# The last group's output-projection rows loaded as two tiles instead of one, in a decode attention block

## The chip, the cores and the metric

One core of a Trainium2 chip runs the whole kernel. The metric is the device time in microseconds (us) of one execution; medians of several runs are given. The profile is of one execution; its span is about 1.8 us shorter than the time, because it leaves out what lies around the first and the last instruction. In the views, PE is TensorE (matrix products), DVE is VectorE, ACT is ScalarE, and SP (SyncE) issues the loads.

Where times from different profiles are compared, they are counted from one event that all kernels share: the start of the last eight products with v ("from the last v" below). Such a figure is the difference of two times that are printed to 0.01 us, so it can be off by 0.01.

## The reference, cut to what matters

```python
h = _layernorm(x) * (1 + ca) + sa
x = x + ga * _A_ref(h, A_k_cache, A_v_cache, A_wq, A_wo)   # attention, 4 x 32 heads, 4096 keys of 128
h = _layernorm(x) * (1 + cb) + sb
x = x + gb * _B_ref(h, B_w_in, B_w_sp, B_b_sp, B_w_out)    # gated MLP
# in _A_ref:  o = softmax(q k^T) v ;  return o.reshape(B, 1, H * Dh) @ wo
# in _B_ref:  z = gelu(x @ w_in); z1 * (w_sp * layernorm(z2) + b_sp) @ w_out
```

The k and v caches are 134 MB each and every byte is used once. They are streamed in 32 steps: eight groups of four heads, times four batch rows. wo, w_in and w_out are small.

## The kernel before: the parts that matter

All large loads are issued on one queue (SP). At the last step the queue gets the last v tile in five parts (1/2, 1/4, 1/8, 1/16, 1/16), then the last group's rows of wo (512 KB), then w_in as two tiles (1344 and 448 KB) and w_out as two tiles (512 and 384 KB):

```python
st["v", i] = load_v(i)                                   # five parts when i is the last step
if i == NQ - 1:
    nc.sync.dma_start(out=st["wo", G - 1], in_=wo_v[G - 1])
    for a, (j0, j1) in enumerate(WJS):
        nc.sync.dma_start(out=win[a], in_=win_v[:, j0:j1, :])
    for a, (j0, j1) in enumerate(JFS):                   # JFS = [(0, 4), (4, 7)]
        nc.sync.dma_start(out=wout[a], in_=wout_v[a])
```

After the last products with v, the attention output oT of the last group meets wo in 16 small products (four heads by four column blocks):

```python
for hl in range(NH):
    for jo in range(J):
        nc.tensor.matmul(attn_ps[:, jo, :], lhsT=wo_g[:, hl, jo * P:(jo + 1) * P], rhs=oT[:, hl, :], ...)
```

What follows is one serial chain of small steps (cut): `x1b` (residual), the second layernorm, `h`; the products with w_in (`z_ps`); gelu, `u`; the third layernorm with an activation table load before its `rstd` (one over the standard deviation); the products with w_out (`y_ps`); `gwb` and `q`, and at the second step of `q` the two branches meet:

```python
for a, (j0, j1) in enumerate(JFS):                       # 28 products: 16 with wout[0], 12 with wout[1]
    ... nc.tensor.matmul(y_ps[:, jo], lhsT=wout[a][...], rhs=u[:, jf], ...)
nc.vector.tensor_tensor(out=gwb, in0=y_ps, in1=gwb, op=ALU.mult)
nc.vector.tensor_tensor(out=q, in0=gwb[:, :, 0], in1=gwb[:, :, 1], op=ALU.add)
nc.vector.tensor_tensor(out=q, in0=q, in1=bc(rstd, J), op=ALU.mult)      # y branch and rstd branch meet
... # add, transpose by one product, copy, and a DMA of the 4 KB output
```

## Time and profile before

| What | Value | Where it is read |
|---|---|---|
| time | 667.54 us, 3 runs (667.51 to 667.61) | the timed runs |
| bytes moved | 283 MB, 425 GB/s over the span | the page |
| last v products start | 653.43 us | timeline |
| products with wo | 654.74 to 655.33 us | timeline |
| last w_out tile lands | 661.26 us (issued 650.96, 10.3 us to landing) | groups by tile |
| last step of q starts | 662.39 us | timeline |
| output issued | 663.57 us | timeline |

The page of the kernel before. Its third part gives, for each DMA queue, packets, MB and share of the 16 DMA engines' time; its fourth the chain of work that ended last, by engine.

```profile
DMA packets 12733, 283.17 MB, mean 425 GB/s; under 512 B 1432, under 2 KB 1952, under 8 KB 4000
...
q1 hardware_dynamic: 12624, 282.73, 98.8%
...
DMA 62%; PE 24%; DVE 12%; ACT 1%; issue 0%; SPq 0%; DVEq 0%
```

The kernel is a stream from HBM. What this change can move lies after the stream's last v bytes. The timeline of that tail (start, duration, engine, line, operation, tiles, number; in brackets what the engine waited for):

```profile
653.43 0.38 PE L363 MATMUL zo_ps<-P_1_109,vt 128*128 128x4 bf16 x8 [0.24 <-DMA vt<-in_A_v_cache_dram]
...
654.74 0.59 PE L400 MATMUL attn_ps<-oT,wo_g 128*128 128x4 bf16 x16 [0.93 <-DMA wo_g<-in_A_wo_dram]
655.37 0.17 DVE L467 TENSOR_TENSOR x1b<-attn_ps,modT 128x16 f32<-128x16 f32 x1 [1.35 <-PE attn_ps L400]
...
658.08 0.17 DVE L479 TENSOR_TENSOR h<-xs,modT 128x16 bf16<-128x16 f32 x1
...
658.40 1.08 PE L492 MATMUL z_ps<-h,win_434 128*128 128x4 bf16 x30 [1.75 <-DVE h L479]
...
659.34 0.35 PE L492 MATMUL z_ps<-h,win_435 128*128 128x4 bf16 x7
...
661.30 0.49 PE L515 MATMUL y_ps<-u,wout_437 128*128 128x12 bf16 x12
...
661.83 0.21 DVE L524 TENSOR_TENSOR gwb<-y_ps,gwb 128x48 f32<-128x48 f32 x1 [0.21 <-PE y_ps L515]
662.07 0.17 DVE L528 TENSOR_TENSOR q<-gwb 128x16 f32<-128x16 f32 x1
662.15 0.20 ACT L171 ACTIVATE rstd_ln_4194<-rstd_ln_4194 128x4 f32<-128x4 f32 x1
...
662.39 0.18 DVE L529 TENSOR_TENSOR q<-q,rstd_ln_4194 128x16 f32<-128x16 f32 x1
```

All 16 products with wo wait for one landing. Near the end two branches run side by side: the y branch (w_out landing, 12 products, gwb, first q) is done at 662.24 and rstd at 662.35. The chain that ended last names the one that released the meeting point (start, duration, what):

```profile
631.94 22.76 DMA wo_g<-in_A_wo_dram
654.69 0.05 issue
654.74 0.60 PE attn_ps L400 x16
...
660.52 1.28 ACT L508
...
661.82 0.31 ACT rstd_ln_4194 L170
...
662.15 0.21 ACT rstd_ln_4194 L171
...
662.39 0.19 DVE q L529
```

Before the change the chain runs from wo through compute and the activation table load (L508) to rstd.

### The profile page before, as it was taken

The page shows a single profiled execution, that of the slowest core. Times are in us where ns is not written, and L with a number is a line of the kernel's source. Part 1 is how long each engine was busy: PE and PEld are TensorE (multiplying, and loading weights), DVE is VectorE, ACT ScalarE, POOL GpSimd, SP SyncE. Part 2 cuts the span into 40 slices and gives each one's busy share as a digit, 9 for nine tenths or more (in the row PEclk, how much of TensorE's full clock was granted, in tenths as well). Part 3 has the DMA queues.
Part 4 walks back from the last instruction along what each step waited for, and adds up shares of the span by engine and source line. Part 5 has one row for each costly group of instructions (what it writes and reads, how often), then busy time and mean ns, then how long its engine had stood idle before and what let it go on. Part 6 is the DMA issues. An engine that isn't in the chain of part 4 may idle for free.

```text
span 665.9 us, 6937 instructions
## 1 busy us (share of the span) xinstructions
PE 410.8 (62%) x3023; PEld 203.3 (31%) x3024; DVE 402.9 (60%) x475; ACT 41.3 (6%) x115; POOL 4.7 (1%) x21
## 2 busy tenths in 40 slices
PE   2557776645676555577665577655566655557774
PEld 2223332222333222233222333222233322223344
DVE  2177766665556665556576556767555757655762
ACT  1200000000000000000000000000000000000002
POOL 2000000000000000000000000000000000000000
PEclk9988876767888667887677887766788766788885
DMA  9999999999999999999999999999999999999995
GB/s 378 433 425 432 438 434 429 427 440 432 429 428 439 432 430 428 437 428 436 429 435 428 436 431 434 426 436 433 434 431 431 434 434 426 437 432 435 426 417 228
DMA packets 12733, 283.17 MB, mean 425 GB/s; under 512 B 1432, under 2 KB 1952, under 8 KB 4000
## 3 DMA queue, kind: packets, MB, share of 16 engines
q1 hardware_dynamic: 12624, 282.73, 98.8%
q8 instruction: 23, 0.38, 0.2%
q14 instruction: 6, 0.05, 0.0%
q0 software_dynamic: 64, 0.00, 0.0%
q10 hardware_dynamic: 16, 0.01, 0.0%
HBM read 282.73 MB, written 0.00 MB: 425 GB/s over the span
## 4 chain that ended last, share of the span: by engine, by line
DMA 62%; PE 24%; DVE 12%; ACT 1%; issue 0%; SPq 0%; DVEq 0%
DMA kt<-in_A_k_cache_dram 58%; PE s_ps L281 23%; DVE kt L276 11%; DMA wo_g<-in_A_wo_dram 3%; SPq L92 0%; PE big L341 0%; PE z_ps L492 0%; DVE S L290 0%; ACT L508 0%; ACT E L311 0%; DVE P_1_109 L314 0%; DVE P_0_105 L314 0%; PE small L155 0%; PE attn_ps L400 0%; DVE mT L300 0%
## 5 line engine op out<-in xcount | busy, mean ns | idle before, releaser
L281 PE MATMUL s_ps<-kt,ident 128*128 128x512 bf16 x1024 | 289.8, 454 | 190.0 <-DVE kt L276 190.0
L276 DVE TENSOR_TENSOR kt<-kt,qbc 128x8192 bf16<-128x8192 bf16 x64 | 282.7, 4420 | 87.3 <-DMA kt<-in_A_k_cache_dram 73.4
L281 PEld LDWEIGHTS <-ident 128*128 128x128 bf16 x1024 | 115.5, 113 | 352.8 <-issue 224.2
L290 DVE TENSOR_REDUCE S<-s_ps 128x64 f32<-128x512 f32 x64 | 44.3, 692 | 120.6 <-PE s_ps L281 120.6
L354 PE MATMUL zo_ps<-sel,osb 128*128 128x4 f32 x248 | 33.1, 257 | 26.6 <-ACT osb L347 26.6
L311 ACT ACTIVATE E<-S,nm 128x128 f32<-128x128 f32 x32 | 12.8, 401 | 564.2 <-DVE nm L308 564.2
L354 PEld LDWEIGHTS zo_ps<-sel,osb 128*128 128x128 f32 x248 | 30.5, 194 | 38.4 <-ACT osb L347 38.4
L341 PE MATMUL big<-vt,P_0_105 128*32 128x512 bf16 x352 | 21.0, 380 | 1.5 <-DMA vt<-in_A_v_cache_dram 1.5
L341 PE MATMUL big<-vt,P_1_109 128*32 128x512 bf16 x320 | 19.1, 381 | 0.0
L341 PE MATMUL big<-vt,P_2_113 128*32 128x512 bf16 x320 | 19.1, 380 | 0.0
L347 ACT COPY osb<-big 128x512 f32<-128x512 f32 x31 | 17.5, 566 | 20.0 <-PE big L341 20.0
L215 PE MATMUL big<-vt,hbc 128*32 128x512 bf16 x128 | 8.9, 445 | 4.9 <-DMA vt<-in_A_wq_dram 4.9
L314 DVE TENSOR_TENSOR P_1_109<-E,mask_99 128x512 bf16<-128x512 f32 x11 | 7.6, 693 | 6.8 <-ACT E L311 6.8
L314 DVE TENSOR_TENSOR P_0_105<-E,mask_99 128x512 bf16<-128x512 f32 x11 | 7.6, 693 | 6.7 <-ACT E L311 6.7
L341 PEld LDWEIGHTS <-P_0_105 128*32 128x32 bf16 x352 | 8.4, 96 | 8.9 <-DMA vt<-in_A_v_cache_dram 1.6
L314 DVE TENSOR_TENSOR P_2_113<-E,mask_99 128x512 bf16<-128x512 f32 x10 | 6.9, 693 | 6.2 <-ACT E L311 6.2
L400 PE MATMUL attn_ps<-oP,wo_g 128*128 128x4 bf16 x112 | 3.8, 165 | 10.5 <-DVE oP L397 10.5
L375 DVE TENSOR_TENSOR oT<-zo_ps,rz 128x4 bf16<-128x4 f32 x32 | 5.4, 168 | 7.4 <-PE zo_ps L363 6.3
L341 PEld LDWEIGHTS <-P_1_109 128*32 128x32 bf16 x320 | 7.6, 96 | 6.7
L341 PEld LDWEIGHTS <-P_2_113 128*32 128x32 bf16 x320 | 7.6, 96 | 6.7
L400 PEld LDWEIGHTS <-wo_g 128*128 128x128 bf16 x128 | 4.3, 97 | 11.5 <-issue 10.4
L308 DVE STREAM_TRANSPOSE nm<-hb 128x32 f32<-128x32 f32 x32 | 6.8, 211 | 1.1
(218 smaller groups left out, 130.7 us busy)
## 6 DMA issues: line engine op xcount, KB each, us to landing
kt<-in_A_k_cache_dram SPq DMA_DIRECT2D x31, 4096.0 KB, 26.0
vt<-in_A_v_cache_dram SPq DMA_DIRECT2D x31, 4096.0 KB, 33.8
vt<-in_A_wq_dram SPq DMA_DIRECT2D x1, 4096.0 KB, 20.4
wo_g<-in_A_wo_dram SPq DMA_DIRECT2D x8, 512.0 KB, 26.2
kt<-in_A_k_cache_dram SPq DMA_DIRECT2D x2, 2048.0 KB, 25.4
vt<-in_w_mod_dram SPq DMA_DIRECT2D x1, 3072.0 KB, 10.1
vt<-in_A_v_cache_dram SPq DMA_DIRECT2D x1, 2048.0 KB, 18.5
win_434<-in_B_w_in_dram SPq DMA_DIRECT2D x1, 1344.0 KB, 24.4
```

Of the source, the lines that this page charges most:

```text
L215: nc.tensor.matmul(qp[hl * R:(hl + 1) * R, 0:n], lhsT=hbc[:, j, b, :], rhs=wv[:, g0:g0 + n, hl, :], start=(j == 0), stop=(j == J - 1), til ...
L276: nc.vector.tensor_tensor(out=kt, in0=kt, in1=q[:, None, :].to_broadcast([P, HT, DH]), op=ALU.mult,)
L281: nc.tensor.matmul(ps, lhsT=ident, rhs=kt[:, :, cc * DC:(cc + 1) * DC], start=(cc == 0), stop=(cc == DH // DC - 1),)
L290: nc.vector.tensor_reduce(out=st["S", i][:, half * HT:(half + 1) * HT], in_=st.pop(("s", i, half)), axis=AX.X, op=ALU.add,)
L308: nc.vector.transpose(out=nm, in_=hb)
L311: nc.scalar.activation(out=E, in_=S, func=AF.Exp, bias=nm[:, 0:1], scale=att_scale, accum_out=rs,)
L314: nc.vector.tensor_tensor(out=P4[:, 0:NT, :], in0=E[:, :, None].to_broadcast([P, NT, NH]), in1=mask4[:, None, :].to_broadcast([P, NT, NH]) ...
L341: nc.tensor.matmul(po[32 * t:32 * t + 32], lhsT=P4[:, n0:n0 + 8, :], rhs=st["v", i][:, n0:n0 + 4, :], start=(u == 0), stop=(u == NU - 1), ...
L347: nc.scalar.copy(out=osb, in_=po)
L354: nc.tensor.matmul(st["o", i], lhsT=osb[:, n, :], rhs=sel[:, NH * n:NH * n + NH], start=(n == 0), stop=(n == 3),)
L375: nc.vector.tensor_tensor(out=oT[:, :, b], in0=st.pop(("o", i)), in1=rz, op=ALU.mult,)
L400: nc.tensor.matmul(attn_ps[:, jo, :], lhsT=wo_g[:, hl, jo * P:(jo + 1) * P], rhs=oT[:, hl, :], start=(g == 0 and hl == 0 and jo == 0), sto ...
```

## The change

The intent: with wo in two tiles of two heads each, the first eight products can run while the second tile is still under way.

```diff
-                            attn_ps[:, jo, :], lhsT=wo_g[:, hl, jo * P:(jo + 1) * P], rhs=oT[:, hl, :],
+                            attn_ps[:, jo, :],
+                            lhsT=(wo_g[:, hl] if g < G - 1 else wo_l[hl // 2][:, hl % 2])[
+                                :, jo * P:(jo + 1) * P],
+                            rhs=oT[:, hl, :],
 ...
+        wo_l = [wk.tile([P, NH // 2, D], BF16, name=f"wo_l{a}", bufs=1) for a in range(2)]
 ...
             if i == NQ - 1:
-                nc.sync.dma_start(out=st["wo", G - 1], in_=wo_v[G - 1])
+                for a in range(2):
+                    nc.sync.dma_start(
+                        out=wo_l[a], in_=wo_v[G - 1, :, a * NH // 2:(a + 1) * NH // 2],
+                    )
```

(The rest of the diff only keeps the old tile for the other seven groups.) The same bytes and the same products; one queue entry more.

More of the change, by code (lines that the diff above doesn't have):

```diff
@@ L384, in apply @@
                 oT = st.pop(("oT", g))
-                wo_g = st.pop(("wo", g))
                 if g < G - 1:
+                    wo_g = st.pop(("wo", g))
                     pp = psum_s.tile([P, NH, B], F32, name="small", bufs=1)
@@ L429 @@
                 g = quads[i][0]
-                st["wo", g] = wk.tile([P, NH, D], BF16, name="wo_g", bufs=2)
                 if g < G - 1:
+                    st["wo", g] = wk.tile([P, NH, D], BF16, name="wo_g", bufs=2)
                     nc.sync.dma_start(out=st["wo", g], in_=wo_w[g])
```

## The prediction

> **What bounds the kernel.** The page's queue part gives the SP queue 98.8% of the DMA time and 425 GB/s over the 665.9 us span: the kernel streams 283 MB, and DMA is 62% of the chain of waits. The instruction orders of both kernels differ only in the last queue entries and in the tile that the last 16 wo products read, so only the last 12 us (654 to 665.9) can move.
>
> **The tail before (timeline).** The last v part lands at about 653.4; oT is ready at 654.02 (653.85 + 0.17). wo_g lands at 654.70 (chain of waits). The 16 products run 654.74 to 655.33 (0.59 us). Then the second layernorm runs serially to h at 658.25, and the win products start at 658.37. Their first weight load waits for h and for the first win tile, which landed at 657.97 (633.57 + 24.4): h released it.
>
> **What the change does.** Same bytes, packets and products; one more DMA. wo took 1.31 us after the last v part, so the first half should land at about 654.05, just as oT is ready. Eight products (about 0.3 us) then run in the wait, and the other eight start at 654.74. attn_ps finishes at about 655.04: 0.29 us saved at the layernorm's start, and h at about 657.97.
>
> **How much survives.** Less, because the transfers behind wo come no earlier:
> - win, first tile, 657.97: h now meets it; products start near 658.08 (-0.29).
> - win, second tile: by bytes between its neighbours' landings about 659.04 (estimate); needed at 659.31 before, 659.02 now: even, 0 to 0.1 us lost.
> - wout, second tile: lands at 661.26 (650.96 + 10.3) and its weight load already started at 661.30, so this end is DMA-bound. y products end 661.79, gwb at 661.83, q at 662.07 to 662.24. The other input, rstd, came at 662.35. An earlier rstd gains only until 662.24: about 0.13 us.
>
> So I expect about 0.1 us: 0.29 us saved, the rest given back in waiting for wout.
>
> **Side effects.** Each queue entry waits for the landing eight entries earlier (instruction order). Now the first win tile waits for the v tile before the last (landed about 643.3) instead of the last k half (633.5). Its issue lasted until 644.02 anyway (10.45 us). The second win tile is issued at about 648.2 instead of 644.07, the wouts at 651 and 652.3 instead of 648.16 and 650.96. Their data flow 6 us later, so the queue should not run dry. The Trainium skill (DMA: Bandwidth & Descriptors, "Anatomy of one DMA") gives a fixed cost of about 2 us per DMA, mostly completion latency. Here it is hidden: the v parts of 512 and of twice 256 KB each filled about 1.23 us per 512 KB, no dearer when split; an extra DMA should cost under 0.05 us.
>
> **Prediction.** 667.4 us (before 667.54), range 666.7 to 668.1. Chances: faster by over 2% 0.005, within 0.99, slower 0.005.
>
> **What would show each step.** Right: two groups of eight wo products, the first starting near 654.1, ahead of the second landing; first x1b product at about 655.07 instead of 655.37; the last y products waiting for wout's second tile; span shorter by 0.05 to 0.2 us. Wrong: the first half landing with the second; win's landing releasing its products over 0.1 us late; wout landing later than 661.3.
>
> **What would make it wrong.** The later issues letting some DMA engines run dry (the windows show DMA share falling to 0.57 from 656 on, so the engines are uneven), delaying win or wout by up to 1 us; or a drift of 0.1% in the whole run's DMA rate, larger than the effect.

## The result, and the profile after

The changed kernel took 667.39 us (667.18 to 667.48, 6 runs), the kernel before beside it 667.51 us (667.38 to 667.61, 6 runs). The ratio is 0.9998 with a 95% interval of 0.9985 to 1.0011: the same.

The timeline of the changed kernel, the lines that answer to those of before:

```profile
653.03 0.37 PE L363 MATMUL zo_ps<-P_1_109,vt 128*128 128x4 bf16 x8 [0.26 <-DMA vt<-in_A_v_cache_dram]
...
653.69 0.37 PE L400 MATMUL attn_ps<-oT,wo_l_438 128*128 128x4 bf16 x8 [0.29 <-DMA wo_l_438<-in_A_wo_dram]
...
654.36 0.38 PE L400 MATMUL attn_ps<-oT,wo_l_439 128*128 128x4 bf16 x8 [0.30 <-DMA wo_l_439<-in_A_wo_dram]
654.78 0.17 DVE L474 TENSOR_TENSOR x1b<-attn_ps,modT 128x16 f32<-128x16 f32 x1 [1.17 <-PE attn_ps L400]
...
657.49 0.17 DVE L486 TENSOR_TENSOR h<-xs,modT 128x16 bf16<-128x16 f32 x1
...
657.81 1.08 PE L499 MATMUL z_ps<-h,win_434 128*128 128x4 bf16 x30 [1.75 <-DVE h L486]
...
658.79 0.38 PE L499 MATMUL z_ps<-h,win_435 128*128 128x4 bf16 x7
...
660.93 0.48 PE L522 MATMUL y_ps<-u,wout_437 128*128 128x12 bf16 x12
...
661.46 0.21 DVE L531 TENSOR_TENSOR gwb<-y_ps,gwb 128x48 f32<-128x48 f32 x1 [0.37 <-PE y_ps L522]
661.63 0.20 ACT L171 ACTIVATE rstd_ln_4196<-rstd_ln_4196 128x4 f32<-128x4 f32 x1
661.70 0.17 DVE L535 TENSOR_TENSOR q<-gwb 128x16 f32<-128x16 f32 x1
...
661.98 0.17 DVE L536 TENSOR_TENSOR q<-q,rstd_ln_4196 128x16 f32<-128x16 f32 x1
```

The chain that ended last, at its end:

```profile
651.74 9.15 DMA wout_437<-in_B_w_out_dram
660.89 0.05 issue
660.93 0.50 PE y_ps L522 x12
661.43 0.02 issue
661.46 0.22 DVE gwb L531
...
661.70 0.18 DVE q L535
...
661.91 0.02 DVEq L536
...
661.98 0.19 DVE q L536
```

The intended overlap is there: two groups of eight, the first 0.67 us ahead of the second. Counted from the last v (653.43 before, 653.03 after), the steps are:

| Step, from the last v | before | after | difference |
|---|---|---|---|
| x1b starts | +1.94 | +1.75 | -0.19 |
| h starts | +4.65 | +4.46 | -0.19 |
| last rstd starts | +8.72 | +8.60 | -0.12 |
| last 12 y products start | +7.87 | +7.90 | +0.03 |
| gwb starts | +8.40 | +8.43 | +0.03 |
| last step of q starts | +8.96 | +8.95 | -0.01 |
| output issued | +10.14 | +10.13 | -0.01 |
| span ends | +12.51 | +12.44 | -0.07 |

The 0.19 us saved at x1b is still there at h, 0.12 of it is left at rstd, and it is gone at q. Between h and rstd the second w_in tile (win_435) takes a part. It landed at 658.75, so the first product that reads it started 0.98 us after the first product with w_in instead of 0.94, and all 56 took 1.93 us instead of 1.85. The rest goes at q: the chain no longer runs through compute but hangs from the last w_out landing, which hardly moved (+7.82 before, +7.86 after). So the products' head start delivered 0.01 us. A further 0.06 us was saved after the output was issued, where the change does no work at all. And the last v itself came 0.40 us earlier in this one pair of profiles. These three needed explaining: is the first absorbed by w_out, what is the second, and is the third caused by the change?

### The profile page after: what moved, and what is told of

It is laid out like the page before. It is cut to its first block, busy times and chain, and to the rows that moved or that the text cites. A ratio compares the mean times of both kernels' runs of the same rounds, so it can differ in the third digit from the quotient of the medians.

```text
span 665.5 us, 6939 instructions
## 1 busy us (share of the span) xinstructions
PE 415.7 (62%) x3024; PEld 204.6 (31%) x3024; DVE 402.6 (61%) x475; ACT 41.3 (6%) x115; POOL 4.7 (1%) x21
## 4 chain that ended last, share of the span: by engine, by line
DMA 62%; PE 24%; DVE 12%; issue 0%; SPq 0%; ACT 0%; DVEq 0%
DMA kt<-in_A_k_cache_dram 58%; PE s_ps L281 24%; DVE kt L276 11%; DMA vt<-in_A_v_cache_dram 3%; DMA wout_437<-in_B_w_out_dram 1%; PE big L341 0%; DVE S L290 0%; ACT E L311 0%; SPq L92 0%; DVE P_1_109 L314 0%; DVE P_0_105 L314 0%; PE y_ps L522 0%; DVE nm L308 0%; DVE mT L300 0%; SPq L78 0%
## 5 line engine op out<-in xcount | busy, mean ns | idle before, releaser
L281 PE MATMUL s_ps<-kt,ident 128*128 128x512 bf16 x1024 | 293.5, 457 | 185.5 <-DVE kt L276 185.5
L215 PEld LDWEIGHTS <-hbc 128*32 128x32 bf16 x128 | 4.4, 114 | 10.3 <-issue 8.4
```

The costliest lines, as they stand in the source:

```text
L215: nc.tensor.matmul(qp[hl * R:(hl + 1) * R, 0:n], lhsT=hbc[:, j, b, :], rhs=wv[:, g0:g0 + n, hl, :], start=(j == 0), stop=(j == J - 1), til ...
L281: nc.tensor.matmul(ps, lhsT=ident, rhs=kt[:, :, cc * DC:(cc + 1) * DC], start=(cc == 0), stop=(cc == DH // DC - 1),)
```

## The experiments

Theory: the tail has two branches of nearly equal length, and the last w_out landing keeps the meeting point where it was. Rivals: another step of the tail absorbs the saving; the timed difference of about 0.12 us comes from the products after all; or it comes from the changed queue (each entry waits for the landing eight entries earlier, so all later entries are issued at other times).

Twelve runs were made, in three sessions, each with five rounds. All gave correct results. The columns from "x1b" on are from the profiles, counted from the last v; all in us. "Last q" is the start of the step where the two branches meet.

| Kernel | its median | before, same session | x1b | last q | span ends | output issue to span end |
|---|---|---|---|---|---|---|
| before_again | 667.72 | 667.68 | +1.92 | +8.95 | +12.51 | 2.38 |
| after_again | 667.59 | 667.68 | +1.74 | +9.20 | +12.70 | 2.31 |
| reverse | 667.48 | 667.68 | +1.95 | +8.96 | +12.46 | 2.33 |
| quarter | 667.90 | 667.68 | +1.68 | +8.99 | +12.65 | 2.48 |
| early_one | 668.52 | 667.55 | +1.98 | +9.00 | +12.57 | 2.38 |
| early_two | 668.41 | 667.55 | +1.82 | +8.82 | +12.32 | 2.31 |
| fine_one | 667.56 | 667.55 | +1.95 | +8.96 | +12.46 | 2.31 |
| fine_two | 667.37 | 667.55 | +1.75 | +8.82 | +12.26 | 2.25 |
| before_c | 667.47 | 667.45 | +1.95 | +8.96 | +12.52 | 2.38 |
| after_c | 667.37 | 667.45 | +1.75 | +8.94 | +12.44 | 2.31 |
| reverse_c | 667.40 | 667.45 | +1.94 | +8.96 | +12.46 | 2.31 |
| fine_two_c | 667.16 | 667.45 | +1.74 | +8.85 | +12.28 | 2.25 |

### Two repeats: before_again and after_again

No edit; each kernel unchanged.

> The kernel before, unchanged, timed against itself: what the comparison shows when nothing changed, and a second profile. Both theories expect a ratio of 1.0000 and medians within 0.1 us of each other. In the profile, counted from the start of the last v products: wo products at +1.31 us, first x1b at +1.94, last q product at +8.96, end of the span at +12.47. If the interval from the second-to-first v landing (0.36 us longer in the first profile of before than in that of after) is chance, it need not repeat here.

> The changed kernel, unchanged, for more rounds and a second profile. My theory (the last wout transfer bounds the end, the saving at x1b is absorbed there): counted from the start of the last v products, first wo products at +0.66 us, second group at +1.33, x1b at +1.75, last q product at +8.95 and span end at +12.47, the same as before within 0.05. Total time 0 to 0.15 us below before. Rival (the products' head start carries through): span end at +12.28 or less.

Against itself the kernel before differed by 0.04 us in the median here and by 0.02 in before_c: that is the size of nothing. The 95% intervals of the ratios are about 0.0013 wide to each side, which is 0.9 us, so no difference of 0.1 us is resolved by the timed runs alone. (The +12.47 of the expectations was worked out from a span rounded to 665.9; with 665.94 it is +12.51.) The changed kernel was 0.09 us faster than before, and its profile showed another end: x1b at +1.74 as expected, but q at +9.20. Here is its line of the timeline for the first products with w_in:

```profile
658.08 2.01 PE L499 MATMUL z_ps<-h,win 128*128 128x4 bf16 x56 [1.92 <-DMA win<-in_B_w_in_dram]
```

h had been ready since 657.76, and the first w_in tile came last. In this execution the transfers after wo landed 0.25 us later than in the first one (why is not shown), and the whole tail followed them: the saving at x1b was not only absorbed but irrelevant. The chain that ended last names again the last w_out tile, not w_in:

```profile
651.79 9.46 DMA wout<-in_B_w_out_dram
661.25 0.05 issue
661.30 0.50 PE y_ps L522 x12
```

### The second tile's products first: reverse and reverse_c

```diff
-                for hl in range(NH):
+                heads = list(range(NH)) if g < G - 1 else [2, 3, 0, 1]
+                for hl in heads:
 ...
```

(The `stop` flag of the products follows the new order.) The queue is that of the changed kernel, but no product can start before the second tile has landed.

> The two transfers of the changed kernel, but the products take the second tile first, so all 16 wait for the last transfer as before the change; the queue is that of the changed kernel. My theory: x1b back at about +1.94 us from the last v products, and the end unchanged at +12.47, total time equal to the changed kernel within 0.1 us. Rival A (the 0.12 us in the medians comes from products running earlier): as slow as before, 667.5. Rival B (it comes from the changed queue): as fast as the changed kernel, 667.4, and the v landings spaced as there.

> Second tile's products first, again, against the changed kernel in the same session. If the products' head start is worth nothing at the end: same time as the changed kernel within 0.06 us. If it is worth the 0.12 us: that much slower.

All 16 products ran in one group again, and x1b was back at +1.95:

```profile
654.58 0.59 PE L401 MATMUL attn_ps<-oT,wo_l 128*128 128x4 bf16 x16 [0.96 <-DMA wo_l<-in_A_wo_dram]
655.20 0.17 DVE L475 TENSOR_TENSOR x1b<-attn_ps,modT 128x16 f32<-128x16 f32 x1 [1.38 <-PE attn_ps L401]
```

Yet reverse took 667.48 us against 667.59 of the changed kernel in one session, and 667.40 against 667.37 in another. The head start is worth nothing at the end, within about 0.1 us either way. What little the changed kernel seems to gain in the timed runs, this one shows too (0.20 and 0.05 us below before), without any overlap.

### The last w_out tile out of the way: early_one and early_two

```diff
         wout = [ ... ]
+        nc.sync.dma_start(out=wout[1], in_=wout_v[1])      # at the head of the stream
 ...
-                for a, (j0, j1) in enumerate(JFS):
-                    nc.sync.dma_start(out=wout[a], in_=wout_v[a])
+                nc.sync.dma_start(out=wout[0], in_=wout_v[0])
```

early_one has wo in one tile, early_two in two.

> The kernel before with the last wout tile (384 KB) loaded at the head of the kernel instead of last. Same bytes in all, so the whole stream of k and v should land about 0.92 us later (384 KB at 425 GB/s). Both theories: slower than before by 0.8 to 0.95 us; counted from the last v products the tail is as before: x1b +1.94, last q product +8.96 (there rstd, not wout, was the later input), end +12.47.

> The same early wout tile, with the split wo tiles. My theory (only the late wout transfer absorbs the saving): with that transfer out of the way the saving of 0.19 us at x1b reaches the end: last q product at +8.77 us from the last v products, end at +12.28, total 0.19 us below early_one. Rival (another step of the tail absorbs it, such as the first win tile or the activation table load): end still at +12.45 or later, total within 0.05 of early_one.

Both were slower than before, by 0.97 and 0.86 us in the medians, because 384 KB now go before the last v. The comparison that counts is between the two. Their last step of q, early_one first:

```profile
663.34 0.17 DVE L529 TENSOR_TENSOR q<-q,rstd_ln 128x16 f32<-128x16 f32 x1 [0.26 <-ACT rstd_ln L171]
```

```profile
663.14 0.18 DVE L536 TENSOR_TENSOR q<-q,rstd_ln 128x16 f32<-128x16 f32 x1 [0.25 <-ACT rstd_ln L171]
```

The last v stood at 654.34 and 654.32. With w_out gone from the end, q waits for rstd in both, and the split moves it by 0.18 us (+9.00 to +8.82), as much as it moves x1b (0.16). Take away the late w_out landing and the saving arrives. The rival that another step absorbs the saving is out as the account of the whole, but not of a part: in these two runs the second w_in tile held nothing (the products with w_in took 1.85 and 1.84 us), in the changed kernel it took 0.08 us. The medians differ by 0.11 us, the means by 0.19; in the profiles the spans end 0.25 us apart, 0.18 at q and 0.07 in the closing sequence explained below.

### Fewer products behind the last landing: fine_one, fine_two and fine_two_c

```diff
-        JFS = [(0, 4), (4, JF)]
+        JFS = [(0, 4), (4, JF - 1), (JF - 1, JF)]
 ...
-            j0, j1 = JFS[jf >= JFS[0][1]]
+            j0, j1 = next(t for t in JFS if jf < t[1])
```

After the last landing only 4 products are left instead of 12. fine_one has wo in one tile, fine_two in two.

> The kernel before with wout in three tiles (4, 2 and 1 chunks), so that 4 instead of 12 products remain after the last landing; wo in one tile. My theory: no gain, since rstd at +8.92 us from the last v products is then the later input of the last q product: q stays at +8.96, end +12.47, total within 0.05 us of before.

> The same three wout tiles with the split wo tiles. My theory: after the last landing only 4 products remain, gwb moves from +8.43 to about +8.2, rstd is at +8.73 to +8.8, so the last q product starts at about +8.8 instead of +8.95 and the end at +12.32: 0.1 to 0.15 us below the changed kernel, 0.15 to 0.25 below before. Rival (the last landing itself, not the products behind it, sets the end, or the added transfer costs as much): no gain over the changed kernel.

> Split wo and three wout tiles, again, against the changed kernel in the same session: end at +12.3 us from the last v products, 0.1 to 0.15 us below the changed kernel and 0.2 to 0.3 below before. If the gain seen earlier was the session's, no difference from the changed kernel.

fine_one gained nothing at q (+8.96) and nothing in time (667.56 against 667.55): there rstd is the later branch, so a shorter y branch is idle gain:

```profile
662.55 0.17 DVE L529 TENSOR_TENSOR q<-q,rstd_ln 128x16 f32<-128x16 f32 x1 [0.26 <-ACT rstd_ln L171]
```

fine_two moved q to +8.82, and its q was released by rstd again:

```profile
661.95 0.17 DVE L536 TENSOR_TENSOR q<-q,rstd_ln 128x16 f32<-128x16 f32 x1 [0.15 <-ACT rstd_ln L171]
```

Each of the two changes alone leaves q where it was, both together move it by 0.14 us. It is not the whole 0.20 us of x1b, since the products with w_in took 0.06 us longer in fine_two (1.91 against 1.85): the second w_in tile again. fine_two took 667.37 against 667.55 of before; in the last session 667.16, against 667.37 of the changed kernel and 667.45 of before. It is the fastest version, ahead of both kernels, though by 0.04% and with an interval that still contains 1 (0.9982 to 1.0007 against before). Of the about 0.15 us between fine_two_c and after_c in the profiles, 0.09 lie before q and 0.06 in the closing sequence explained below.

### Four tiles: quarter

```diff
-        wo_l = [wk.tile([P, NH // 2, D], ...) for a in range(2)]
+        wo_l = [wk.tile([P, 1, D], ...) for a in range(NH)]
 ...
-                for a in range(2):
+                for a in range(NH):
 ...
```

> Four tiles of one head each, two more transfers. My theory: x1b at about +1.6 us from the last v products (four products after the last landing instead of eight), the last wout still lands at about +7.9, end at +12.4 to +12.5, total within 0.1 us of the changed kernel. Rival (each added transfer, and the later issue of win and wout that comes with it, costs time): win issued only after the second v part (about 650.5 us) and the wouts after 652, so some DMA engines run dry, wout lands 0.3 us or more later, and the time rises by that.

x1b came at +1.68, 0.07 us earlier than with two tiles. The rival was half right. w_in was issued only at about 650.9 us, and the DMA share fell. The windows of quarter, then of the changed kernel (us; busy time and number of each engine; granted clock; DMA share; GB/s):

```profile
649.00:651.00 2.00, 1.37 (x52) 1.28 (x49) 0.00 (x0) 0.00 (x0) 0.00 (x0) 0.57 0.78 300
651.00:653.00 2.00, 1.70 (x55) 1.53 (x56) 0.00 (x0) 0.00 (x0) 0.00 (x0) 0.50 0.83 243
```

```profile
649.00:651.00 2.00, 1.42 (x54) 1.34 (x51) 0.00 (x0) 0.00 (x0) 0.00 (x0) 0.50 1.03 413
651.00:653.00 2.00, 1.52 (x45) 1.27 (x42) 0.00 (x0) 0.00 (x0) 0.00 (x0) 0.50 1.04 403
```

In the first window the share is 0.78 where the changed kernel has 1.03, so some DMA engines ran dry; yet the last w_out products started at +7.94 instead of +7.90. That the engines that ran dry were not those that land last is an inference from this. q came at +8.99, and the time was 667.90 against 667.68 of before (not clear of noise: the interval is 0.9989 to 1.0015). Against the changed kernel of the session (667.59) it is 0.31 us, and 0.17 us of such a difference lies, in the profiles, after the output's issue (2.48 against 2.31).

### What the last 2.3 us are: read from all profiles

The last column of the table falls into four narrow groups, and they follow the number of queue entries. At the end SP checks the semaphores, those of the DMAs among them, two at a time and always in the same order. The starts of these checks, as the trace records them (the one that holds the output's semaphore is in brackets; it passes when the output has landed):

```
            output issued, landed   checks on SP                                         closing begins
before      663.57  664.94          663.98 664.04 664.10 [664.95] 665.01 665.07          665.14
after       663.16  664.52          663.57 663.64 663.70 663.76 [664.54] 664.60          664.67
fine_two    663.14  664.50          663.55 663.62 663.68 663.74 663.80 [664.52]          664.58
quarter     663.62  664.98          664.04 [664.10, ends 665.01] 665.04 665.10 665.17 665.23   665.29
```

One check takes 0.06 us. The output needs 1.36 to 1.37 us to land in all four, and checks that stand before its own are done meanwhile; those behind it come on top. The kernels hand out eight semaphores in turn, so each added queue entry moves the output's semaphore by one. With as many entries as before it is in the fourth check (2.37 to 2.38 us, four profiles), with one more in the fifth (2.31 to 2.33, seven profiles), with two more in the sixth (2.25, two profiles), and with three more, in quarter, back in the second (2.48, one profile). fine_one has one entry more without the change to wo, and shows the same. So one of the things the change did was to move the output's semaphore by one check, for 0.06 us. It would be lost again at a different count.

### The earlier v: before_c and after_c

No edit. In the first two profiles of before, the second part of the last v landed 2.79 and 2.85 us after the first; in the eight of other kernels 2.43 to 2.46.

> The kernel before a third time. Open: is the 0.3 us by which its last v part landed later after the v tile before it (10.09 and 10.15 us in two profiles, 9.79 to 9.85 in the eight of the other kernels) its own, or chance? Queue theory: again 10.1 us, and the interval between the first and second last-v landings again 2.8 us. Chance theory (an instruction fetch delays one DMA engine, and it matters only if that engine is among the last): either value, here near 9.8 and 2.45 as often as not. Time equal to before within 0.1 us.

> The changed kernel a third time, in one session with the three others. Tail as in the first profile: first wo products at +0.66 us from the last v products, x1b +1.75, end +12.47 (or +12.66 as in the second profile, if a DMA engine is late again and win's landing releases its products). Interval between the first and second last-v landings 2.43 us by the queue theory, 2.43 or 2.8 by chance. Time 0.1 to 0.2 us below before.

before_c showed 2.43 us, like all the others: the earlier v is not an effect of the change, and the queue theory falls here. fine_one had already pointed there, for up to then its queue is that of before.

The trace shows what makes the difference. A DMA adds 16 increments to its semaphore as its engines finish, so there are 16 landing times for each part of v. Sorted, counted from the span's start:

```
before,   v part 1:  643.37 643.43 643.57 643.75 644.04 644.10 644.51 | 646.18 646.64 646.93 647.29 647.71 647.77 647.79 647.96 648.15
before,   v part 2:  645.81 645.88 646.03 646.20 646.52 646.54 646.96 | 648.64 649.06 649.69 650.15 650.16 650.23 650.37 650.56 650.94
before_c, v part 1:  643.30 643.43 643.67 643.73 643.76 643.92 644.18 | 646.26 646.40 646.56 647.02 647.68 647.70 647.84 647.98 648.23
before_c, v part 2:  645.76 645.86 646.12 646.18 646.25 646.37 646.63 | 648.70 649.00 649.47 650.12 650.14 650.27 650.37 650.43 650.65
```

Seven engines run 3.6 to 4.8 us ahead of the last, and a tile has landed only with its slowest engine. From part 1 to part 2, 15 engines of before can be paired off with steps of 2.39 to 2.48 us. One is left over, from 646.93 to 650.94: 4.01 us. (The trace does not name the engines: one landing of each part is left out, so that the other 15, taken in order, have steps as equal as possible.) In the other 13 profiles the best such pairing leaves out one engine at 3.94 to 4.02 us, with the others at 2.39 to 2.50; in some, the left-out landing could as well be one or two places earlier or later. In before and before_again that engine came in last, 0.38 and 0.41 us behind the next, so everything behind it was late; in before_c it went from 646.40 to 650.37 and came in 14th of 16, which delayed nothing. In the other profiles it was 11th to 15th, but for fine_two_c, where it was last by 0.05 us. Beside the queue of the kernel's loads only one thing moved in that time. The queues of before between 646 and 648 us (packets, MB, share):

```profile
q1 hardware_dynamic: 183, 0.78, 95.8%
q8 instruction: 1, 0.02, 2.8%
```

That packet is 16 KB of instructions, it took 0.88 us, and one starts at this point (646.6 to 648.3 us) in all 14 profiles. That the fetch is what holds the one engine up by about 1.55 us is an inference from the timing, since the trace does not name the engine. No run was made to test it, and none shows why it fell on the last engine twice.

## Why the prediction was right or wrong, point by point

**The number: right.** 667.4 was forecast and 667.39 measured, and the difference was in the noise, as the chances said. But the sum behind it was not right: of the 0.07 us by which the profile became shorter, counted from the last v, 0.01 came by the forecast path. The match of "about 0.1 us" is luck.

**The overlap: right, its size too large.** "Eight products (about 0.3 us)", 0.29 us saved. The first group did start at +0.66 ("near 654.1" was expected, which is +0.67). But x1b gained 0.19, not 0.29. The error was to take half of 0.59 us for half the products. Sixteen took 0.59 us and eight 0.37 to 0.38, so one product more costs about 0.026 us, and the rest is paid once per group: 8 x 0.026 = 0.21 us is what can be hidden. The Trainium skill (TensorE: Matmul & The Clock Gate, "Wait — 56ns, not 53.3ns?") says that the start-to-start time of matmuls never drops below about 25 ns however small they are, and this trace agrees with it: after the first pair these products start 26 to 28 ns apart. The rest of such a group, about 0.17 us here, is the recorded length of one product (0.166 to 0.167 us) and does not shrink with the number.

**Where the saving stops: right.** The prediction said that w_out's second tile makes this end DMA-bound and takes back most of the gain. The chain of waits of the changed kernel hangs from that tile, and early_two showed the saving arriving once it is gone from the end.

**What is left of it: the step that failed.** "An earlier rstd gains only until 662.24: about 0.13 us." It was 0.01. The term took the end of the first q step, 662.24, as the moment when the second could start. But from the first of these two steps to the second the trace of the changed kernel needs 0.28 us from start to start (661.70 to 661.98): a step of 0.17 us and then a gap, in which a wait of its own stands (DVEq L536). So counted from 662.07 the second could not start before 662.35, where it already stood at 662.39. That left 0.04 us, and of this the w_out products, 0.03 us later from the last v, took nearly all. (before_c and after_c agree: gwb at +8.41 and +8.42, q at +8.96 and +8.94, so 0.02 us.) A gap of 0.1 us between one step's end and the next step's start was left out of a slack of 0.13; the prediction's own inputs, 662.35 and 662.24, make it 0.11.

**The gain that was measured.** From the last v to the end of the span, 0.07 us: 0.01 from the products and 0.06 from the closing checks, which the prediction did not have. reverse and reverse_c have the second without the first and end at +12.46, against +12.44 (after, after_c) and +12.51 to +12.52 (three profiles of before). The medians' differences, 0.12, 0.09 and 0.08 us, are a little above 0.07. The rest, 0.01 to 0.05, is about as large as what the kernel before shows against itself (0.04), and is left open.

**The side effects: right.** The first w_in tile was issued at 643.21 (643.3 forecast), the second at 648.07 (648.2), the w_outs at 650.51 and 651.74 (651 and 652.3), and the queue did not run dry (share 1.03 and 1.04 in the windows above). An extra DMA "should cost under 0.05 us": the second half of wo started its products at +1.33, against +1.31 for the whole tile. With three more entries, in quarter, the queue did run dry, so that worry was sound but two entries early.

**The w_in meeting points: right.** The first tile was to meet h, and it does: h decides in the first profile, the landing in after_again. The second was called "even, 0 to 0.1 us lost", and it took 0.08 us in the first profile. Neither decides the end as long as w_out comes later; in fine_two, where rstd decides, the second tile costs 0.06 us.

## What to carry to other kernels

Before a wait in a tail is shortened, list every branch that meets behind it with its arrival time, and count slack from start to start of the steps, not from end to start: here two branches lay within 0.1 us, and each change alone gave nothing while both together gave 0.14 us at the meeting point. That slack is not made of the steps' lengths alone: look for waits between them. Halving a group of small products does not halve its time, because part of it is paid per group. When the effect looked for is below what the kernel shows against itself, let a version that has everything of the change except its intended effect (here: the second tile's products first) decide what the difference is made of.

## What the Trainium skill lacked or had wrong

- Instruction fetches beside a saturated stream. Runtime: NRT & Kernel Launch, "Instruction fetch mechanics", says that instructions are refilled in 16 KiB blocks and calls the cost mostly hidden. The block size agrees (one packet of 16384 bytes). But in all 14 profiles one DMA engine needed 3.94 to 4.02 us where the others needed 2.39 to 2.50, at the time of such a fetch, and where that engine came in clearly last, in 2 of the 14, the load landed about 0.4 us later. That the fetch is the cause is inferred from the timing.
- Spread of the DMA engines. DMA: Bandwidth & Descriptors, "Latency and other measured facts", has two engines (7 and 15) as usually slower, and takes that to be specific to DMAs whose descriptors GpSimd makes. The loads here are issued by SP, and nine of the 16 increments of a load come late: in the first v part of before the seventh is at 644.51, the eighth at 646.18 and the last at 648.15 us, 4.8 us behind the first. The trace does not name the engines, so whether 7 and 15 are among the nine is not shown. The page's account of the 16 increments ("Why a DMA increments its semaphore by 16 and not by 1") is what makes this readable, and agrees with the trace.
- The closing checks. No page that I found has it: the program ends with SP checking semaphores two at a time in fixed order, 0.06 us each, and where the output's semaphore stands among them is worth 2.25 to 2.48 us from issue to end.
- Gaps between dependent vector steps on 128x16 tiles: 0.28 us from start to start for an instruction of 0.17 us, in the two q steps of the changed kernel, where a separate wait stands between them; 0.21 us from xs to h (657.28 to 657.49), where none does. I did not find a page with these numbers, and the gap was the size of the slack in question.
